# A fused retention and ELU layer: the last 2048 tokens in two blocks of 1024 instead of four of 512, with the first weight's pieces streamed from DRAM

## The chip, the cores and the metric

The kernel runs on one core of a Trainium2 chip. The metric is device time in microseconds (us) of one execution; lower is better. All engines work through queues of instructions in order: TensorE (PE, with its weight loads PEld), VectorE (DVE), ScalarE (ACT), GpSimd (POOL) and SyncE (SP), which here issues all the DMAs.

## The reference

Retention over 4 batches, 8 heads, 768 positions and 64 dimensions, then a layer of two products with an ELU between them, all in fp32:

```python
gamma = 1.0 - 2.0 ** (-5.0 - np.arange(H))
for t in range(S):
    state = gamma * state + einsum('bhd,bhe->bhde', k[:, :, t], v[:, :, t])
    y[:, :, t] = scale * einsum('bhd,bhde->bhe', q[:, :, t], state)
x = y.transpose(0, 2, 1, 3).reshape(3072, 512)
h = x @ w_in                                # 512 x 2048
g = where(h > 0, h, exp(min(h, 0)) - 1)
out = g @ w_out                             # 2048 x 512
```

## The kernel before

**Blocks.** The 3072 tokens are worked off in six blocks of 512 (`tb` 0 to 5). For each, the retention gives x (in chunks of 128 tokens: `scores`, `states`, `outputs_step`, gathered in `retention_step`, with small 64x64 matmuls), then come the "first" (x @ w_in and ELU) and the "second" (g @ w_out). The two products are done after Strassen and Winograd: seven products of half-size blocks instead of eight, with sums of blocks before (on DVE) and after (on ACT, which copies a product out of PSUM, and DVE, which adds the next to it). Block 0 is done plainly at first, block 1 has a one-level first (`first`, products L758). For blocks 2 to 5 (loop L1363) the first is one-level in five of its seven products (`first_rest`, L923, 256 columns) and two-level in two of them, j = 2 and 3 (`first_twice`, L870, 128 columns). The second of blocks 1 to 5 is two-level throughout (`second_twice`, L953): seven outer products in the order 1, 2, 6, 7, 5, 3, 4 (`ORDER2`), each with seven inner ones of four matmuls 128 columns wide (L973).

**Weights.** Blocks and sums of w_in lie in SBUF to the end (`w_a`, `w_b`, `w_s`); `first_rest` reads them there. The 49 pieces of w_out and the four sums for each of j = 2, 3 of w_in are computed once, stored to DRAM scratch, and fetched again for each block as pieces of 128x512 (256 KB) into a ring of 11 tiles named `wq` (`fetch_small`, L809): whenever a product has used its piece, the next fetch is issued on SP. The ring is opened after the staging tiles `stage` (named `wi` where sums are staged) are closed, in the same SBUF space. The sums of w_in are made by `combine_small` (L833) during block 1's first, and each j is stored by one DMA of 1 MB (L657, `send_small`).

**Order.** The order of the instructions is written by hand. Work of the next block (chunk loads `bring`, the scaling of v L286, the retention steps, x combinations L468) is put between the products of the current one; the second's last products are left as a `tail` to the next block's first. ELU (`elu`, L491 to L495) is Relu and Exp on ACT and one operation on DVE, which `later` defers. A DMA on SP waits for the one eight DMAs earlier.

**Steps touched.** `lift` and `plus` (L895, L899) take the two-level products out of PSUM, `first_end` (L939) adds and starts the ELU, `next_input` (L782 ff.) builds the second's inputs in place, `input_parts` makes the four differences of each outer product (L847), and `sum_up` adds outer products and stores the output.

Of the kernel before, what the change touches and what calls it, by code (L numbers as in the profile page):

```python
# [18 lines left out]
def kernel(  # L19
# [6 lines left out]
    scratch3: bass.AP,  # L26
    out: bass.AP,
# [47 lines left out]
    mpool = ctx.enter_context(tc.tile_pool(name="mpool", bufs=4))  # L75
    hpool = ctx.enter_context(tc.tile_pool(name="hpool", bufs=4))
    epool = ctx.enter_context(tc.tile_pool(name="epool", bufs=2))
    small = ctx.enter_context(tc.tile_pool(name="small", bufs=6))
# [5 lines left out]
    stage = early.enter_context(tc.tile_pool(name="stage", bufs=3))  # L84
    t4 = early.enter_context(tc.tile_pool(name="t4", bufs=1))
# [188 lines left out]
    x_of = lambda tb: xt_.rearrange("p j a t -> p j (a t)") if tb == 1 else xb  # L274
# [516 lines left out]
    RING = 11  # L791
    TWICE = [2, 3]
    SMALL = {5: 0, 6: 1, 7: 2, 3: 3}
    small_w, to_fetch, before = [], [], []
    for tb in range(1, NTB):
        for j in TWICE if tb > 1 else []:
            m1, m2, *mine = [(tb, 0, j, k) for k in (1, 2, 6, 7, 5, 4, 3)]
            to_fetch += [m1] + before[:1] + [m2] + mine[:2] + before[1:] + mine[2:3]
            before = mine[3:]
        to_fetch, before = to_fetch + before, []  # L800
        for j in ORDER2:
            last = (4, 3) if j == 4 and tb == NTB - 1 else (3, 4)
            mine = [(tb, 1, j, k) for k in (1, 2, 6, 7, 5) + last]
            to_fetch += mine[:2] + before + mine[2:5]
            before = mine[5:]
        to_fetch, before = to_fetch + before, []
    to_fetch = [x for x in to_fetch if x[1] == 1 or x[3] in SMALL]

    def fetch_small():  # L809
        if not to_fetch:  # L810
            return
        name = to_fetch.pop(0)
        _, which, j, k = name
        t = ring.tile([P, 4, P], FP32, name="wq", tag="wq")
        if k in SMALL:
            n = SMALL[k]
            nc.sync.dma_start(
                t.rearrange("p f d -> p (f d)"), (scratch2[SEVEN[j]] if which else scratch3[j - 1])[:, 512 * n : 512 * n + 512]
            )
        else:  # L820
            q = 4 * SLOT[j] + {1: 0, 2: 1, 4: 3}[k]
            nc.sync.dma_start(t.rearrange("p f d -> p (f d)"), scratch[q])
        small_w.append((name, t))


    W_IN = {2: w_a_[:, :, :, 1], 3: w_s_[:, :, 2]}

    def combine_small(j):

        t = stage.tile([P, 4, 4, P], FP32, name="wi", tag="stage")  # L830
        a11, a12, a21, a22 = (W_IN[j][:, 2 * r : 2 * r + 2, :, c, :] for r in range(2) for c in range(2))
        s1, s2, s3, s4 = (t[:, k].rearrange("p (n f) c -> p n f c", f=2) for k in range(4))
        tt = lambda o, x, y, op: nc.vector.tensor_tensor(out=o, in0=x, in1=y, op=op)  # L833
        tt(s1, a21, a22, ALU.add)
        yield
        tt(s2, s1, a11, ALU.subtract)
        yield
        tt(s3, a11, a21, ALU.subtract)
        yield
        tt(s4, a12, s2, ALU.subtract)  # L840
        to_send.append((scratch3[j - 1], t.rearrange("p k f d -> p (k f d)")))
# [3 lines left out]
    def quarters_of_input(t, b11, b12, b21, b22):  # L845

        sub = lambda o, x, y: nc.vector.tensor_tensor(out=o, in0=x, in1=y, op=ALU.subtract)  # L847
        sub(t[:, 0], b12, b11)
        yield
        sub(t[:, 1], b22, t[:, 0])  # L850
        yield
        sub(t[:, 2], b22, b12)
        yield
        sub(t[:, 3], b21, t[:, 1])

    def combine_x_twice():

        t = tpool.tile([P, 4, 2, 2, P], FP32, name="ts", tag="ts")
        b = [xb[:, 2 + k].rearrange("p (h t c) -> p t h c", h=2, t=2)[:, u] for k in range(2) for u in range(2)]
        for _ in quarters_of_input(t[:, :, 0], *b):  # L860
            pass
        for n, j in enumerate(TWICE):
            b11, b12, b21, b22 = (x[:, n] for x in b)
            s1, s2, s3, s4 = (t[:, k, 0, n] for k in range(4))
            xs[j] = {1: b11, 2: b21, 3: b22, 4: s4, 5: s1, 6: s2, 7: s3}


    PLACE = {2: "C11", 3: "C12"}

    def first_twice(tb, j):  # L870

        dst = PLACE[j]
        place = lambda name, r, t: gq[name][:, 4 * r : 4 * r + 4, P * t : P * t + P]
        full = lambda t: t.rearrange("p a (b c) -> p (a b) c", c=P)

        def product(k, ps, begin):
            if k in SMALL:
                name, w = small_w.pop(0)
                assert name == (tb, 0, j, k)
                lhs = [w[:, f, :] for f in range(4)]  # L880
            else:
                r, c = {1: (0, 0), 2: (0, 1), 4: (1, 1)}[k]
                lhs = [W_IN[j][:, 2 * r + f // 2, f % 2, c, :] for f in range(4)]
            for f in range(4):
                nc.tensor.matmul(  # L885
                    ps[:, f, :], lhsT=lhs[f], rhs=xs[j][k], start=(begin and f == 0), stop=True,
                    skip_group_check=True,
                )
            if k in SMALL:
                fetch_small()  # L890

        def lift(ps, o=None):
            if o is None:
                o = full(mpool.tile([P, 2, TH], FP32, name="m", tag="m"))
            nc.scalar.copy(o, ps)  # L895
            return o

        def plus(r, t, ps, m):
            nc.vector.tensor_tensor(out=place(dst, r, t), in0=ps, in1=m, op=ALU.add)  # L899

        pa = full(bank("a"))
        product(1, pa, True)
        m1 = lift(pa)
        yield
        pb = full(bank("b"))
        product(2, pb, True)
        plus(0, 0, pb, m1)
        product(6, pa, False)
        u2 = lift(pa)
        pd = full(bank("d"))  # L910
        product(7, pd, True)
        m7 = lift(pd)
        yield
        product(5, pa, False)
        plus(1, 1, pa, m7)
        yield
        product(4, pd, False)
        plus(1, 0, pd, u2)
        yield
        product(3, pa, False)  # L920
        lift(pa, place(dst, 0, 1))

    def first_rest(n, j, ps):  # L923

        w, x = {
            1: (w_a[n][:, :, 0], xb[:, 0:2, half[0]]), 6: (w_s[n][:, 0], xt[1]), 5: (w_b[n][:, :, 0], xt[0]),
            4: (w_b[n][:, :, 1], xt[3]), 7: (w_s[n][:, 1], xt[2]),
        }[j]
        for fi in range(2):
            for j2 in range(2):  # L930
                nc.tensor.matmul(  # L931
                    ps[:, fi, :], lhsT=w[:, fi, j2, :], rhs=x[:, j2, :],
                    start=(j in (1, 7) and fi == 0 and j2 == 0), stop=(j2 == 1), skip_group_check=True,
                )

    def first_end(n, name, ps, x=None):

        g = gq[name][:, 2 * n : 2 * n + 2, :]
        nc.vector.tensor_tensor(out=g, in0=ps, in1=g if x is None else x, op=ALU.add)  # L939
        g = g.rearrange("p a b -> p (a b)")  # L940

        def combine():
            mine = lambda x: gq[x][:, 2 * n : 2 * n + 2, :].rearrange("p a b -> p (a b)")
            sub = lambda o, x, y: nc.vector.tensor_tensor(out=o, in0=x, in1=y, op=ALU.subtract)
            sub(mine("T3"), mine("C22"), mine("C12"))
            if n < NQ - 1:
                sub(mine("T1"), mine("C12"), mine("C11"))
            else:
                later.append(lambda: sub(mine("T1"), mine("C12"), mine("C11")))

        return lambda: elu(g, g, 3, combine if name == "C22" else None)

    def second_twice(tb, behind_last):  # L953
# [7 lines left out]
        def input_parts(j):  # L961
            x, t = gq[INPUT2[j]], tpool.tile([P, 4, 4, P], FP32, name="ts", tag="ts")
# [6 lines left out]
        def product(j, k, ps, begin):  # L969
            name, w = small_w.pop(0)  # L970
            assert name == (tb, 1, j, k)
# [5 lines left out]
            fetch_small()  # L977
# [34 lines left out]
        def inner_end(j):  # L1012

            res = hpool.tile([P, 2, 2, P], FP32, name="res", tag="h")
            to = out[tb, 1, 0].rearrange("p d (t c) -> p d t c", t=2)
            k = kept2[7].rearrange("p (d t c) -> p d t c", d=2, t=2)
            pa = bank("a")[:, 0, 0:P]
            product(j, 1, pa, True)
            m1 = copy(pa)
            pb = bank("b")[:, 0, 0:P]  # L1020
            product(j, 2, pb, True)
            add(res[:, 0, 0], pb, m1)
            yield
            product(j, 6, pa, False)
            u2 = copy(pa)
            pd = bank("d")[:, 0, 0:P]
            product(j, 7, pd, True)
            m7 = copy(pd)
            yield
            add(u2, u2, k[:, 1, 0])  # L1030
            add(u2, pd, u2)
# [479 lines left out]
```

## Time and profile before

| | |
|---|---|
| three runs | 632.44 to 634.4 us, median 634.11 us |
| profiled execution, span | 631.6 us |
| DVE, ACT, POOL busy | 76%, 40%, 4% of the span |
| moved by DMA | 136.32 MB, 216 GB/s in the mean |
| pieces `wq` fetched | 277 of 256 KB, landing 4.4 us after issue |
| chunks fetched | 22 of 1 MB, landing 8.7 us after issue |

A line of the timeline has the start, the time to the end of the last instruction, engine, line, operation, output <- input, tile shapes and number of instructions. An fp32 matmul leaves two records. "gC" and "ts" are the input blocks of the second and their sums, pa to pd are PSUM banks; `gT` is the tile of T3.

### The profile page before, as it was taken

To read this page: it belongs to the slowest core of one execution; us is meant where nothing else is said; L and a number is where in the kernel's file an instruction comes from. 1 tells how busy PE (TensorE), PEld (TensorE's weight loads), DVE (VectorE), ACT (ScalarE), POOL (GpSimd) and SP (SyncE) were. 2 spreads that over 40 slices of the span, in tenths; PEclk is the share of its full clock that TensorE was granted. 3 is DMA by queue.
4 is the path that set the end of the run, shared out by engine and by line. 5 is a ranking of instruction groups with operands and counts; after the bars stand their busy time and mean duration, and the time that the engine had idled before them with its cause. 6 is when DMAs were issued, how large, how long until landed. Compare 5 with 4: busy or idle time off the path is not lost.

```text
span 631.6 us, 16140 instructions
## 1 busy us (share of the span) xinstructions
PE 623.8 (99%) x6678; PEld 560.5 (89%) x6678; DVE 482.1 (76%) x882; ACT 255.3 (40%) x476; POOL 22.1 (4%) x30
## 2 busy tenths in 40 slices
PE   8999999999999999999999999999999999999997
PEld 6864578888899999888999989999989999988997
DVE  6688789989799665799585589777489877558975
ACT  6798646025541114553112646112465211366311
POOL 1021000000000000200000100000110000000000
PEclk9999999999999999999999999999999999999999
DMA  8698669699288788306888702889810698700794
GB/s 329 260 416 295 186 202 268 196 272 319 113 266 257 234 258 315 141 2 199 257 258 296 278 2 71 268 280 289 317 64 16 220 310 252 207 17 4 239 309 151
DMA packets 75897, 136.32 MB, mean 216 GB/s; under 512 B 6320, under 2 KB 31792, under 8 KB 70832
## 3 DMA queue, kind: packets, MB, share of 16 engines
q1 hardware_dynamic: 75824, 135.29, 64.9%
q8 instruction: 53, 0.87, 0.5%
q14 instruction: 20, 0.16, 0.1%
HBM read 114.03 MB, written 21.23 MB: 214 GB/s over the span
## 4 chain that ended last, share of the span: by engine, by line
PE 98%; DVE 0%; issue 0%; ACT 0%
PE pa L973 20%; PE pa L931 10%; PE pd L973 10%; PE pb L973 5%; PE pa L885 5%; PE pb L931 4%; PE pa L758 4%; PE pa L535 3%; PE qa L931 3%; PE x L625 3%; PE pd L885 2%; PE qd L931 2%; PE pd L931 2%; PE pd L758 2%; PE pa L625 2%; PE kv L352 2%
## 5 line engine op out<-in xcount | busy, mean ns | idle before, releaser
L981 ACT COPY ms<-pa 128x128 f32<-128x128 f32 x104 | 27.6, 265 | 148.2 <-PE pa L973 148.2
L973 PE MATMUL pa<-ts,wq 128*128 128x128 f32 x560 | 74.2, 275 | 0.0
L973 PE MATMUL pd<-ts,wq 128*128 128x128 f32 x552 | 73.5, 276 | 0.0
L973 PEld LDWEIGHTS pa<-ts,wq 128*128 128x128 f32 x560 | 68.5, 192 | 0.4
L973 PEld LDWEIGHTS pd<-ts,wq 128*128 128x128 f32 x552 | 67.1, 192 | 0.6 <-DVE res L985 0.2
L973 PE MATMUL pa<-gC,wq 128*128 128x128 f32 x480 | 64.6, 278 | 0.0
L492 ACT ACTIVATE r<-r 128x512 f32<-128x512 f32 x96 | 60.5, 631 | 3.1
L973 PEld LDWEIGHTS pa<-gC,wq 128*128 128x128 f32 x480 | 59.0, 192 | 1.3
L491 ACT ACTIVATE r<-gC 128x512 f32<-128x512 f32 x64 | 39.9, 624 | 31.9 <-DVE gC L939 31.9
L985 DVE TENSOR_TENSOR res<-pd,ms 128x128 f32<-128x128 f32 x68 | 19.5, 287 | 39.6 <-PE pd L973 38.4
L495 DVE SCALAR_TENSOR_TENSOR gC<-r,gC 128x512 f32<-128x512 f32 x64 | 42.6, 697 | 0.7 <-ACT r L492 0.7
L847 DVE TENSOR_TENSOR ts<-gC,ts 128x512 f32<-128x512 f32 x60 | 41.3, 688 | 1.0
L847 DVE TENSOR_TENSOR ts<-gC 128x512 f32<-128x512 f32 x60 | 41.0, 683 | 0.0
L286 POOL TENSOR_TENSOR chunk<-chunk,vf 128x512 f32<-128x512 f32 x16 | 19.4, 1212 | 429.6 <-DMA chunk<-in_qkv_dram 429.6
L973 PE MATMUL pb<-gC,wq 128*128 128x128 f32 x240 | 31.7, 275 | 0.0
L1006 ACT COPY res<-pa 128x128 f32<-128x128 f32 x34 | 9.0, 265 | 55.1 <-PE pa L973 55.1
L973 PEld LDWEIGHTS pb<-gC,wq 128*128 128x128 f32 x240 | 29.2, 192 | 0.0
L704 ACT COPY m<-pa 128x512 f32<-128x512 f32 x24 | 14.0, 582 | 33.0 <-PE pa L758 18.7
L939 DVE TENSOR_TENSOR gC<-qa,gC 128x512 f32<-128x512 f32 x8 | 5.5, 692 | 25.0 <-PE qa L931 18.3
L931 PE MATMUL pa<-xt,w_s 128*128 128x256 f32 x96 | 23.0, 382 | 0.0
L931 PE MATMUL pa<-xt,w_b 128*128 128x256 f32 x96 | 23.0, 382 | 0.0
L931 PE MATMUL pa<-xb,w_a 128*128 128x256 f32 x96 | 22.7, 379 | 0.0
(262 smaller groups left out, 1247.4 us busy)
## 6 DMA issues: line engine op xcount, KB each, us to landing
wq<-scratch_dram SPq DMA_DIRECT2D x277, 256.0 KB, 4.4
chunk<-in_qkv_dram SPq DMA_DIRECT2D x22, 1024.0 KB, 8.7
wraw<-in_w_dram SPq DMA_DIRECT2D x15, 1024.0 KB, 6.0
out_dram<-res SPq DMA_DIRECT2D x14, 256.0 KB, 4.1
scratch_dram<-gT SPq DMA_DIRECT2D x12, 256.0 KB, 4.3
scratch_dram<-m SPq DMA_DIRECT2D x12, 192.0 KB, 6.1
scratch_dram<-so SPq DMA_DIRECT2D x4, 512.0 KB, 4.7
scratch_dram<-wi SPq DMA_DIRECT2D x2, 1024.0 KB, 6.5
```

Of the source, the lines that this page charges most:

```text
L286: eng.tensor_tensor(out=v, in0=v, in1=vf[:, i].unsqueeze(2).to_broadcast([C, H, D]), op=ALU.mult)
L491: nc.scalar.activation(e, h, AF.Relu, scale=-1.0)
L492: nc.scalar.activation(e, e, AF.Exp, scale=-1.0)
L495: nc.vector.scalar_tensor_tensor(g, e, -1.0, h, ALU.add, ALU.max)
L625: nc.tensor.matmul(X[j][:, d, :], lhsT=w[j][:, d * P : d * P + P], rhs=x[j], start=(n == 0 and d == 0), stop=at_end, skip_group_check=True,)
L758: nc.tensor.matmul(ps[:, fi, :], lhsT=w[:, fi, j2, :], rhs=x[:, j2, :], start=(begin and fi == 0 and j2 == 0), stop=(j2 == 1), skip_group_ ...
L847: sub = lambda o, x, y: nc.vector.tensor_tensor(out=o, in0=x, in1=y, op=ALU.subtract)
L885: nc.tensor.matmul(ps[:, f, :], lhsT=lhs[f], rhs=xs[j][k], start=(begin and f == 0), stop=True, skip_group_check=True,)
L931: nc.tensor.matmul(ps[:, fi, :], lhsT=w[:, fi, j2, :], rhs=x[:, j2, :], start=(j in (1, 7) and fi == 0 and j2 == 0), stop=(j2 == 1), skip_ ...
L973: nc.tensor.matmul(ps, lhsT=w[:, f, :], rhs=ts[j][k][:, f, :], start=(begin and f == 0), stop=(f == 3), skip_group_check=True,)
L981: nc.scalar.copy(m, ps)
L985: nc.vector.tensor_tensor(out=o, in0=x, in1=y, op=ALU.add)
```

## The change

Blocks 2, 3 and blocks 4, 5 are merged to two blocks of 1024 tokens (`NB` = 2). In them the second's matmuls are 256 columns wide (`second_big`), the two-level products of the first also (`big_twice`, four passes in the order of `ORDER1`), and its other five products 512 (`big_rest`).

The larger tiles need room. So w_in no longer stays in SBUF: during block 1's first, all pieces of it are stored to DRAM (`send_quarters`: twelve DMAs of 128 KB; `send_layer`: twenty of 256 KB; `combine_small` sends six DMAs for each j instead of one), and `w_a`, `w_b`, `w_s` become tiles for g (`G`). All weights of the large blocks are then fetched as pieces from `scratch3`, `scratch4` and the scratches of w_out, into a ring of 8 slots (for block 1's second 14). The pools `mpool`, `hpool`, `small` are closed after block 1 and two larger ones opened.

Block 1's second runs to its end before the first large block begins. The retention steps lie at other places (`VISITS`): block 3's are inside two passes of `big_twice`, blocks 4 and 5 inside the first `second_big`; chunks of blocks 3 and 5 are loaded four at once. The output's layout changes, and the host puts it in order.

```diff
-    RING = 11
-    TWICE = [2, 3]
...
+    def fetch():
+        while wanted and slots:
+            name, source = wanted.popleft()
+            slot = slots.popleft()
+            nc.sync.dma_start(slot[:, 0 : source.shape[1]], source)
+            where[name] = slot
+
+    def done(name):
+        slot = where.pop(name)
+        if slot in kept_slots or wanted and wanted[0][0][0] == 1:
+            slots.append(slot)
+        fetch()
...
-        to_send.append((scratch3[j - 1], t.rearrange("p k f d -> p (k f d)")))
+        for at in range(2):
+            to = scratch3[j - 2, at]
+            mine = t[:, :, 2 * at : 2 * at + 2].rearrange("p k f d -> p k (f d)")
+            to_send.append((to[1].rearrange("p (k c) -> p k c", k=2), mine[:, 1:3]))
+            to_send.append((to[2][:, 0:256], mine[:, 0]))
+            to_send.append((to[3][:, 0:256], mine[:, 3]))
+
+    def send_quarters(j):
+
+        for at in range(2):
+            for k, n, half in ((1, 0, 0), (2, 0, 1), (4, 2, 1)):
+                r, c = {1: (0, 0), 2: (0, 1), 4: (1, 1)}[k]
+                to_send.append((
+                    scratch3[j - 2, at, n][:, 256 * half : 256 * half + 256].rearrange("p (f d) -> p f d", f=2),
+                    W_IN[j][:, 2 * r + at, :, c, :],
+                ))
...
+    def send_layer(j, ns):
+
+        for n in ns:
+            to_send.append((
+                scratch4[PLANE[j], n].rearrange("p (f c) -> p f c", f=2), LAYER[j][:, n].rearrange("p f k c -> p f (k c)")
+            ))
...
+    def big_layer_x():
+
+        sub = lambda o, x, y: nc.vector.tensor_tensor(out=o, in0=x, in1=y, op=ALU.subtract)
+        b11, b12, b21, b22 = (x[:, 2 * r : 2 * r + 2] for r in range(2) for x in (xa, xb2))
+        t1, t2, t3, t4_ = (next_ts().rearrange("p (k t) -> p k t", k=2) for _ in range(4))
+        layer_x.update({1: b11, 5: t1, 6: t2, 7: t3, 4: t4_})
+        sub(t1, b12, b11)
+        yield
+        sub(t2, b22, t1)
+        yield
+        sub(t3, b22, b12)
+        yield
+        sub(t4_, b21, t2)
...
+    def big_twice(n, j, at):
...
+            for f in range(2):
+                nc.tensor.matmul(
+                    ps[:, f, :], lhsT=w[:, f * P : f * P + P], rhs=big_xs[j][k], start=(begin and f == 0), stop=True,
+                    skip_group_check=True,
+                )
+            if half or k == 3:
+                done(name)
...
+        pa = bank("a")
+        product(1, pa, True)
+        m1 = lift(pa)
+        yield
+        pb = bank("b")
+        product(2, pb, True)
+        plus(0, 0, pb, m1)
+        product(6, pa, False)
+        u2 = lift(pa)
+        pd = bank("d")
+        product(7, pd, True)
+        m7 = lift(pd)
+        yield
+        product(5, pa, False)
+        plus(1, 1, pa, m7)
...
+    def big_end(m, name, ps, x=None):
+
+        g = G[name][m // 4][:, m % 4, :]
+        nc.vector.tensor_tensor(out=g, in0=flat(ps), in1=g if x is None else flat(x), op=ALU.add)
...
+    def next_big_input(j):
+
+        x, op = {2: ("T3", ALU.add), 6: ("C21", ALU.subtract)}[j]
+        for r in range(2):
+            for q in (slice(0, 2), slice(2, 4)):
+                nc.vector.tensor_tensor(out=G["C11"][r][:, q], in0=G[x][r][:, q], in1=G["C11"][r][:, q], op=op)
...
@@ -1331,15 +1553,34 @@
+        if n == 0:
+            send_quarters(2)
+            send_layer(1, range(NQ))
+            send_layer(4, range(NQ))
+        elif n == 1:
+            for j in (6, 7, 5):
+                send_layer(j, range(NQ))
+            send_quarters(3)
         send_small()
...
-    for _ in range(RING):
-        fetch_small()
-
-    sec = second_twice(1, combine_x_twice)
+    ring_ = ctx.enter_context(tc.tile_pool(name="ring", bufs=1, side="right")).tile([P, 8, 512], FP32, name="wq")
...
+    fetch()
+
+    sec = second_twice(1, lambda: run(big_x(2)))
...
+    for nb in range(NB):
...
+        for at, (j, sub) in enumerate(ORDER1):
+            if at == 2:
+                rest(0, 1)
+            cur = big_twice(nb, j, sub)
             next(cur)
-            next(tail, None)
-            next(parts, None)
+            if at:
+                next(tail, None)
+            else:
+                run(tail)
             next(cur)
...
+            if at == 0 and nb == 0:
+                retention_step(3, 0)
+            elif at == 1:
+                if nb == 0:
+                    retention_step(3, 2)
+                    next(tail)
+                    retention_step(3, 3)
+                    for _ in tail:
+                        pass
+                    retention_step(3, 4)
+                some(xparts, 4)
+            elif at == 2:
+                some(xparts, 2)
+                if more:
+                    bring(groups[0], 0)
+            elif at == 3:
+                run(xparts)
+                if more:
+                    bring(groups[0], 1)
+            if at == 2:
+                big_end(0, "C11", qa[0])()
...
+        VISITS = [(0, "end"), (1, "middle"), (1, "end"), (3, "end"), (4, "middle"), (4, "end"), (5, "middle"), (5, "end")]
         for s in sec:
...
+            if more and at in VISITS:
+                n = VISITS.index(at)
+                if n < 3:
+                    retention_step(groups[0], n + 2)
+                    if n == 1:
+                        for m in range(CPB):
+                            bring(groups[1], m)
+                else:
+                    retention_step(groups[1], n - 3)
```

## The prediction

> **What bounds the kernel now.** I read the page from the top: busy shares, slices, chain, groups; then stretches of the trace where the change works. First the shares and the chain of waits that ended last.
>
> ```profile
> PE 623.8 (99%) x6678; PEld 560.5 (89%) x6678; DVE 482.1 (76%) x882; ACT 255.3 (40%) x476; POOL 22.1 (4%) x30
> PEclk9999999999999999999999999999999999999999
> PE 98%; DVE 0%; issue 0%; ACT 0%
> ```
>
> TensorE is busy for 623.8 of 631.6 us at full clock, and the chain is TensorE all the way. So a gain must be time of PE itself, and any wait put into PE's queue is paid in full. Next, PE's pitch. The means of one in the groups (275 ns at 128 columns, 382 ns at 256) overlap their neighbours and can't be divided; the timeline gives starts of whole products.
>
> ```profile
> 190.51 1.06 PE L973 MATMUL pd<-ts,wq 128*128 128x128 f32 x8
> 191.40 1.06 PE L973 MATMUL pa<-ts,wq 128*128 128x128 f32 x8
> ...
> 132.64 1.89 PE L758 MATMUL pa<-xt,w_a 128*128 128x256 f32 x8
> 134.37 1.89 PE L758 MATMUL pb<-xt,w_a 128*128 128x256 f32 x8
> ...
> 37.31 3.60 PE L535 MATMUL pa<-xb,w_a 128*128 128x512 f32 x8
> 40.74 3.60 PE L535 MATMUL pa<-xb,w_b 128*128 128x512 f32 x8
> ```
>
> Eight records are four matmuls. Start to start: 0.893 us, so 223.3 ns each at 128 columns; 1.727 us, 431.6 ns at 256; 3.43 us, 858 ns at 512. Twice the width costs 1.93 and 1.99 times as much: wide matmuls save only the small rest.
>
> **What the change removes.** Per pair of blocks the two-level second goes from 2x196 matmuls of 128 columns to 196 of 256; for four blocks 784 become 392, each saving 2x223.3-431.6 = 15.0 ns: 5.9 us. The two-level products of the first (224 become 112) save 1.7 us, its other five products (320x431.6 become 160x858) 0.8 us. Together 8.4 us. The largest idle of PE before, 1.25 us at 298 us in L423 (an output product of the retention), is at a place that is rearranged: taken as gone. A gain of 9.7 us; bounds 8.4 and 9.7. DVE and ACT work half as many, twice as wide operations; that would be a gain only if they bounded.
>
> The Trainium skill, page "TensorE: Matmul & The Clock Gate", section Back-to-back issue gap, gives for sustained streams about 81 ns a matmul at 128 columns and 131 at 512. By that (98 at 256, an estimate) the 175 us of 784 narrow products would shrink by some 69 us; the 223.3 and 431.6 ns above contradict the ratio, and the measurement decides.
>
> **What it adds: a later first fetch (step A).** Pieces for the stages after it can be fetched only when the ring's tiles, which overlie the staging tiles, are free, so when the last store from `wi` has landed. The queue before:
>
> ```profile
> 146.50 0.47 SPq L110 DMA_DIRECT2D chunk<-in_qkv_dram  x1
> 147.66 0.33 SPq L657 DMA_DIRECT2D scratch_dram<-wi  x1
> 148.10 1.09 SPq L110 DMA_DIRECT2D chunk<-in_qkv_dram  x2
> 168.19 0.33 SPq L657 DMA_DIRECT2D scratch_dram<-wi  x1
> 173.33 0.80 SPq L822 DMA_DIRECT2D wq<-scratch_dram  x2
> ...
> 177.53 1.05 PE L973 MATMUL pa<-gC,wq 128*128 128x128 f32 x8
> ```
>
> And what the DMA engines moved, in slices of 1.425 us from 125 us:
>
> ```profile
> GB/s 290 285 285 284 287 335 116 210 318 230 351 289 349 179 236 284 228 276 247 443 425 414 431 414 109 0 0 0 0 0 98 379 264 12 65 338 286 236 346 404
> ```
>
> The bytes run out at about 159.3 us; the last `wi` leaves at 168.19 (its inputs on DVE, L833, end then) and takes until about 173.1; the first fetch, issued at 173.33, can have landed at about 175.5, and PE wants it at 177.53. The changed queue has, ahead of that fetch, 12 quarter stores of 128 KB and 20 layer stores of 256 KB more: 1.57+5.24 = 6.8 MB, while the two 1 MB `wi` stores become six each. At 350 GB/s these take 19.4 us. Cover: 8.9 us idle (159.3 to 168.2), 1.8 us because the last `wi` overlaps others instead of running alone, 2.0 us of slack on PE. So PE stalls 19.4-12.7 = 6.7, say 7 us. The rate is not shown for this mix: 425 GB/s (the chunk loads at 152 to 158) would give 3.3 us; 258 GB/s (eight DMAs in flight of 192 KB landing in 6.1 us, the row scratch<-m) 13.7. Most bytes are 256 KB stores, landing in 4.3 us (gT), nearer the first: 350. Behind the late SP queue also stand two chunk loads, whose scaling (L286) waits on DVE; that lies under the same PE stall.
>
> The page "DMA: Bandwidth & Descriptors", sections Bandwidth and Rules for kernel authors, asks for 1 MiB a DMA and measures 138 GB/s at 64 KB against 341 at 1 MB, so it speaks against cutting the stores. At 200 GB/s, an estimate between, the 6.8 MB would be 34 us and the stall 21.
>
> **Small ones.** Chunk loads come four at once (4.2 MB, 9.9 us at 425 GB/s) where they came singly. With 13 pieces ahead of block 3's at 0.893 us each, 11.6 us, less 2 us of landing: 0.6 us short; for block 5's seven pieces of 1.73 us, 12.1 us, are enough. 0.6 (0 to 4). The handover where pools are closed: 0.25 (0 to 0.5). The retention of block 3, four steps within one pass instead of over a block: the next products wait for DVE's scaling of y (L398): 0.8 (0 to 1.5). The last sum and store, 128x512 for 128x128: 0.5.
>
> **Step E: the fourth pass of `big_twice`.** Before, the ELU of the first C11 follows all lifts on ACT, and only x combinations of 512 columns stand beside it:
>
> ```profile
> 244.33 0.68 DVE L468 TENSOR_TENSOR xt<-xb,xt 128x512 f32<-128x512 f32 x1
> 246.60 0.69 DVE L939 TENSOR_TENSOR gC<-qa,gC 128x512 f32<-128x512 f32 x1 [1.59 <-ACT gC L895]
> ...
> 245.98 0.58 ACT L895 COPY gC<-pa 128x512 f32<-128x512 f32 x1 [0.31 <-PE pa L885]
> 247.32 0.63 ACT L491 ACTIVATE r<-gC 128x512 f32<-128x512 f32 x1 [0.76 <-DVE gC L939]
> 247.99 0.63 ACT L492 ACTIVATE r<-r 128x512 f32<-128x512 f32 x1
> ```
>
> Now DVE has, in this order: plus(1,1) of the third pass; two subtractions of `big_layer_x` (128x1024); C11's add (`big_end`). ACT has behind that add its Relu and Exp, and only then the lift of m1 of the fourth pass, which PE's product 6 needs to reuse the bank. With t=0 where product 5 of the third pass ends: DVE 0.7 + 2x1.13 + 0.7 = 3.7 us (from 128x128 0.287, 128x256 0.42, 128x512 0.685 a column step of 1.04 ns is read, 1.13 spaced for 1024), ACT 2x0.63+0.58 and handovers to 5.7. PE has three products for that time (1, 4, 2), 6x431.6 ns = 2.6 us. Stall 3.1, in both blocks: 6.2 us (5 to 7). Nothing stands behind it that PE could do; DVE catches up in it.
>
> **Step F: `second_big` of the first block with retention inside.** At product 2 the `seen` copy stands behind four `next_big_input` sums (4x1.13 against 3.5 us of PE work): 0.4. At product 5 the state sums go at the middle, behind four sums and half the input parts: 2.0. At product 3 the `across` matmuls wait behind three dependent 128x1024 sums (1.25 each) and four subtractions: 2.0. Together 4.4 (2 to 6). Before, the same sums were 0.7 us and retention stood at other places.
>
> **Sum.** 631.6-9.7+7.0+0.6+0.25+0.8+6.2+4.4+0.5 = 641.7 as a span. The profiled execution is 2.5 us under the median 634.1, so as a run **644 us**.
>
> **Rivals.**
> (1) Faster: the stores drain at 425 GB/s and the DVE and ACT waits of E and F hide. For it: the DMA engines were idle 9 us here and DVE is busy 76% only. Against: E's chain is in order on two queues, so half of it at the least must go by a wrong duration. With A 3.3 and half of E, F and of the small ones: 634.1-9.7+3.3+5.3+1.1 = 634.1; with A nil, E and F at a fifth and the small ones at half: 627.6. It ends faster only if A+E+F come to less than 6 us.
> (2) DMA decides: small stores at 258 GB/s (A 13.7), chunk bursts 4 us late: 644+6.7+3.4 = 654. For it: 192 KB stores landing in 6.1 us. Against: 256 KB in 4.3.
> (3) No change: gain and waits cancel, A 3.3 with E and F at half, 634 as above.
> (4) The wide matmuls don't gain what is said, because a 256-column product is held up by its piece, 256 KB in 1.73 us (152 GB/s); then 644+8.4 = 652. Before, 261 GB/s ran beside the 128-column products from 180 to 200 us with PE busy for 20.00 of 20.00 us, so hardly.
>
> **How the numbers follow.** This kernel's three runs span 0.3%, so the bound for a change that can be told is 0.3%, 1.9 us: 632.2 to 636.0. Forecast and its neighbourhood (636 to 650): 0.62; rival 2 and 4: 0.10; rival 3: 0.10; rival 1: 0.18. Slower 0.72, same 0.10, faster 0.18. Range 631 to 652: it lets out most of rival 1 and the worst of rival 2.
>
> **What would show it.** A: the first 128-column product of the two-level second in block 1 waits for a DMA, PE idle 3 to 14 us near 178. E: PE idle about 3 us at product 6 of the fourth pass, twice, ACT's lift of m1 behind Relu and Exp. F: idle of 2 us before y products in the first large second. Products of 256 columns at 1.73 us each. I am wrong if the first fetch lands before 178, or if DVE at 128x1024 is shorter than 1.1 us.

## The result, and the profile after

| | before | after |
|---|---|---|
| median of four runs each, same chip | 633.52 us (632.44 to 634.40) | 657.99 us (655.32 to 659.90) |
| ratio, 95% interval | | 1.0392 (1.0359 to 1.0425): slower |
| span of the profiled execution | 631.6 us | 654.8 us |
| PE busy | 623.8 us | 623.8 us |
| moved by DMA | 136.32 MB | 126.67 MB |

The direction was forecast, the size was not: 24.5 us slower, where the forecast of 644 was 10 above the median known then, and the time lies outside the range of 631 to 652. The page of the changed kernel, first the shares, the clock in 40 slices and the chain of waits:

```profile
PE 623.8 (95%) x5350; PEld 469.5 (72%) x5350; DVE 470.8 (72%) x730; ACT 245.9 (38%) x420; POOL 24.4 (4%) x30
PEclk9999999999969989989999999999999999999999
PE 85%; DVE 6%; DMA 6%; issue 1%; SPq 1%; ACT 1%; DVEq 0%; ACTq 0%
```

The chain is no longer PE alone: DVE and DMA have 6% each. PE is idle for 31.0 us (654.8-623.8), before 7.8. And the clock, full throughout before, has three slices below 9. The timeline of PE shows where (the number in brackets is the idle time before the line and what ended it):

```profile
176.43 1.89 PE L761 MATMUL pa<-xb,w_b 128*128 128x256 f32 x8
188.17 2.05 PE L911 MATMUL pa<-gC,wq 128*128 128x128 f32 x8 [9.85 <-DMA wq<-scratch_dram]
190.01 1.92 PE L911 MATMUL pb<-gC,wq 128*128 128x128 f32 x8
...
235.74 1.33 PE L911 MATMUL pa<-w_a,wq 128*128 128x128 f32 x8 [2.85 <-DMA wq<-scratch_dram]
236.86 1.92 PE L911 MATMUL pa<-gC,wq 128*128 128x128 f32 x8
...
288.13 2.08 PE L1111 MATMUL pa<-ts,wq 128*128 128x256 f32 x4 [2.97 <-ACT m L1121]
405.09 1.99 PE L1202 MATMUL pa<-gC,wq 128*128 128x256 f32 x8 [0.80 <-DMA wq<-scratch_dram]
435.44 1.55 PE L411 MATMUL y<-chunk 64*64 64x64 f32 x62 [1.48 <-DVE chunk L367]
453.80 0.69 PE L426 MATMUL y<-chunk 64*64 64x64 f32 x32 [1.62 <-DVE seen L395]
494.01 1.13 PE L1111 MATMUL pa<-ts,wq 128*128 128x256 f32 x4 [2.91 <-ACT m L1121]
```

These seven waits add up to 22.5 us, and the steps A (188), chunk loads (235, 405), E (288, 494) and F (435, 454) are all there. Not foreseen is what follows some of them: from 188.17 to 190.01 four matmuls of 128 columns take 1.84 us, twice the 0.893 of before. The view by stretches gives PE's busy time (second number), and after the engines the clock, the DMA share and GB/s:

```profile
186.00:188.00 2.00, 0.00 (x0) 0.00 (x0) 1.03 (x2) 0.00 (x0) 0.00 (x0) 0.50 0.71 259
188.00:190.00 2.00, 1.83 (x8) 1.86 (x9) 0.00 (x0) 0.00 (x0) 0.00 (x0) 0.50 0.73 181
190.00:192.00 2.00, 2.00 (x11) 2.00 (x10) 0.00 (x0) 0.27 (x1) 0.00 (x0) 0.50 0.96 239
192.00:194.00 2.00, 2.00 (x10) 1.70 (x10) 0.89 (x2) 0.14 (x1) 0.00 (x0) 0.96 1.00 373
```

After the wait PE works at half clock for nearly 4 us; the clock had fallen near 182 us, during the wait. Summed over stretches of 2 us, PE's busy time times the missing share of clock comes to 5.2 us: 2.0 after 188 us, 1.7 after 235, 1.5 after 288. After 494 the clock stayed at 1.00.

### The profile page after: what moved, and what is told of

Same layout as the page of the kernel before. It is cut to its first block, busy times and chain, and to the rows that moved or that the text cites. A ratio compares the mean times of both kernels' runs of the same rounds, so it can differ in the third digit from the quotient of the medians.

```text
span 654.8 us, 13105 instructions
## 1 busy us (share of the span) xinstructions
PE 623.8 (95%) x5350; PEld 469.5 (72%) x5350; DVE 470.8 (72%) x730; ACT 245.9 (38%) x420; POOL 24.4 (4%) x30
## 2 busy tenths in 40 slices
DMA packets 76010, 126.67 MB, mean 193 GB/s; under 512 B 5936, under 2 KB 40496, under 8 KB 71216
## 4 chain that ended last, share of the span: by engine, by line
PE 85%; DVE 6%; DMA 6%; issue 1%; SPq 1%; ACT 1%; DVEq 0%; ACTq 0%
PE pa L1202 13%; PE pa L1154 11%; PE pd L1202 6%; DMA wq<-scratch_dram 5%; PE pa L1111 4%; PE pb L1154 4%; PE pa L761 4%; PE pb L1202 4%; PE pa L538 3%; PE x L628 3%; PE pd L1154 3%; PE pa L911 3%; PE pa L628 2%; PE pd L1111 2%; PE y L411 2%; PE pd L761 2%
## 5 line engine op out<-in xcount | busy, mean ns | idle before, releaser
L1202 PE MATMUL pd<-ts,wq 128*128 128x256 f32 x120 | 28.3, 379 | 0.0
L1202 PE MATMUL pa<-gC,wq 128*128 128x256 f32 x112 | 26.8, 382 | 0.8 <-DMA wq<-scratch_dram 0.8
L1202 PE MATMUL pa<-ts,wq 128*128 128x256 f32 x112 | 26.7, 381 | 0.0
L1154 PE MATMUL pa<-ts,wq 128*128 128x512 f32 x56 | 26.5, 596 | 0.0
L1154 PE MATMUL pa<-xt,wq 128*128 128x512 f32 x56 | 26.3, 592 | 0.0
L1154 PE MATMUL pa<-w_s,wq 128*128 128x512 f32 x56 | 26.3, 592 | 0.0
L707 ACT COPY m<-pa 128x512 f32<-128x512 f32 x26 | 15.1, 582 | 29.4 <-PE pa L761 18.8
L1202 PEld LDWEIGHTS pd<-ts,wq 128*128 128x128 f32 x120 | 22.8, 190 | 3.1
L1202 PEld LDWEIGHTS pa<-gC,wq 128*128 128x128 f32 x112 | 21.0, 190 | 4.5 <-DMA wq<-scratch_dram 1.2
L1111 PE MATMUL pa<-ts,wq 128*128 128x256 f32 x64 | 18.1, 407 | 5.9 <-ACT m L1121 5.9
L1202 PEld LDWEIGHTS pa<-ts,wq 128*128 128x128 f32 x112 | 21.1, 190 | 3.4 <-issue 0.5
L911 PE MATMUL pa<-gC,wq 128*128 128x128 f32 x72 | 11.6, 312 | 10.2 <-DMA wq<-scratch_dram 9.8
```

The source lines that it names most:

```text
L707: nc.scalar.copy(m, ps)
L911: nc.tensor.matmul(ps, lhsT=w[:, f, :], rhs=ts[j][k][:, f, :], start=(begin and f == 0), stop=(f == 3), skip_group_check=True,)
L1111: nc.tensor.matmul(ps[:, f, :], lhsT=w[:, f * P : f * P + P], rhs=big_xs[j][k], start=(begin and f == 0), stop=True, skip_group_check=True,)
L1154: nc.tensor.matmul(flat(ps), lhsT=w[:, k, :], rhs=layer_x[j][:, k, :], start=(j in (1, 7) and k == 0), stop=(k == 1), skip_group_check=True,)
L1202: nc.tensor.matmul(ps, lhsT=w[:, f, :], rhs=ts[j][k][:, f, :], start=(begin and f == 0), stop=(f == 3), skip_group_check=True,)
```

## The experiments

Three things had to be told apart: whether the waits come from where the prediction put them, whether the half clock comes from the waits and costs what it seems to, and whether the wide matmuls gain anything once the waits are gone. The ratio behind each is against the kernel before on the same chip.

**1. The stores alone, in the kernel before.** The extra 32 stores are added at the changed kernel's places; `fetch_small`, the ring and the narrow matmuls stay.

```diff
+        if n == 0:
+            send_quarters(2)
+            send_layer(1, range(NQ))
+            send_layer(4, range(NQ))
+        elif n == 1:
+            for j in (6, 7, 5):
+                send_layer(j, range(NQ))
+            send_quarters(3)
         send_small()
```

> The kernel before, with the change's 32 extra stores of w_in (6.8 MB) put at the same places of the queue, and nothing else; what they store is never read. Theory (the stores hold back the first fetch): in the changed kernel PE idled 9.85 us there and then ran some 4 us at a clock of 0.50, so about 2 us more; here 633.5+12 = 645 us, PE idle 8 to 11 us near 178 us, and a fetch as what ends it. Rival (the new ring and its tiles, or the changed places of retention, hold back the first product; stores pass in the idle time of the DMA engines): 633 to 635 us, no idle there.

Measured: 644.73 us, ratio 1.0181 (1.0161 to 1.0200). Its PE timeline, and SP's at the same place:

```profile
176.40 1.89 PE L760 MATMUL pa<-xb,w_b 128*128 128x256 f32 x8
188.71 2.05 PE L995 MATMUL pa<-gC,wq 128*128 128x128 f32 x8 [10.41 <-DMA wq<-scratch_dram]
...
174.97 0.38 SPq L659 DMA_DIRECT2D scratch_dram<-wi  x1
185.47 0.80 SPq L824 DMA_DIRECT2D wq<-scratch_dram  x2
```

The stores alone make the wait, 10.41 us, and 11.9 us of time (632.87 us was the median of before beside it), as expected; neither the changed ring and pools nor the moved retention is needed for it. The first fetch leaves at 185.47 us, before at 173.33.

**2. The first C11's ELU behind the lifts.**

```diff
             elif at == 2:
-                some(xparts, 2)
+                elu_later = big_end(0, "C11", qa[0])
+                some(xparts, 1)
...
             elif at == 3:
+                elu_later()
                 run(xparts)
...
-            if at == 2:
-                big_end(0, "C11", qa[0])()
```

(The second wide difference moves into the fourth pass.)

> The changed kernel with the first C11's add and ELU moved behind the lifts of the fourth pass of the two-level first, and the two 1024-wide x differences there set apart. Theory (that ELU stands ahead of the lift of m1 in ACT's queue): the two waits of 2.97 and 2.91 us near 287 and 493 us go, and the half clock after the first (1.5 us) with them: 7 us less than the changed kernel's 658, 651 us. Rival (the bank is late because of DVE's wide differences, whatever ACT does): the waits stay within 1 us of what they were, 656 to 658.

Measured: 650.74 us, ratio 1.0276 (1.0248 to 1.0303). In ACT's timeline of the changed kernel the lift stands behind Relu and Exp, which stand behind DVE's add:

```profile
286.31 0.63 ACT L494 ACTIVATE r<-w_a 128x512 f32<-128x512 f32 x1 [4.01 <-DVE w_a L1164]
286.97 0.63 ACT L495 ACTIVATE r<-r 128x512 f32<-128x512 f32 x1
287.51 0.57 ACT L1121 COPY m<-pa 128x512 f32<-128x512 f32 x1
```

With the ELU moved, the same lift comes first, and product 6 follows product 2 at PE's own pitch:

```profile
287.23 0.58 ACT L1121 COPY m<-pa 128x512 f32<-128x512 f32 x1 [1.22 <-PE pa L1111]
...
287.83 1.03 PE L1111 MATMUL pb<-xb,wq 128*128 128x256 f32 x4
288.70 1.03 PE L1111 MATMUL pa<-ts,wq 128*128 128x256 f32 x4
```

Both waits are gone; 7.25 us between the medians. The edit moved one wide difference as well, so the time alone does not separate the ELU from the rival of DVE's wide differences. The rows do: the lift itself waits only for PE's product (PE pa above), and in the changed kernel it came last because Relu and Exp stood ahead of it on ACT, held by DVE's add. DVE's wide differences act through that add, not by themselves.

**3. Chunk loads one at a time.**

```diff
-                        for m in range(CPB):
-                            bring(groups[1], m)
...
+            singly = [(1, "middle"), (2, "first"), (2, "middle"), (3, "first")]
+            if more and at in singly:
+                bring(groups[1], singly.index(at))
```

(And block 3's loads likewise, one at the middle of each of the third to sixth outer products.)

> The changed kernel with the chunk loads of blocks 3 and 5 issued one at a time, over four places each, instead of four at once. Theory (4.2 MB at once hold back the pieces behind them): the wait of 2.85 us near 234 us and that of 0.80 us near 404 us go, and about 1.7 us of half clock after the first: 5 us less, 653 us. Rival (the ring of 14 slots is too short for a piece in 0.893 us whatever stands between): the wait near 234 us moves but stays over 2 us, 656 to 658.

Measured: 656.79 us, ratio 1.0367 (1.0331 to 1.0403), which does not separate it from the changed kernel. The waits for pieces near 235 and 405 us are gone, as the theory says, so the ring was not too short. But a new one of 1.97 us came near 417 us: block 5's scores, for its last chunk (L315). That, a first wait of 10.27 us in this execution instead of 9.85, and 0.7 us more of half clock behind it gave some 3 of the 5 us back.

**4. PE kept busy through the first wait.**

```diff
+    def keep_busy(count):
+        for n in range(count):
+            nc.tensor.matmul(fill, lhsT=line[:, 0:P], rhs=line[:, P : P + 512], start=True, stop=True, skip_group_check=True)
...
+    keep_busy(11)
```

> The changed kernel with 11 matmuls of 512 columns (11x0.858 = 9.4 us) on constants, read by nobody, put on PE just ahead of the first product that waits for a piece near 178 us. Theory (after an idle time PE runs at half clock for a while): the wait is then filled, the granted clock near 188 to 192 us is 1.00, and the time falls by some 2 us, to 656. Rival (the clock falls at that place for another reason, the load on DMA or memory): clock 0.50 at 188 to 192 us again, and no gain: 658.

Measured: 658.98 us, ratio 1.0410 (1.0382 to 1.0438), no gain.

```profile
178.70 9.61 PE L1588 MATMUL fill<-etab 128*128 128x512 f32 x22
189.40 1.13 PE L911 MATMUL pa<-gC,wq 128*128 128x128 f32 x8 [1.10 <-DMA wq<-scratch_dram]
190.37 1.06 PE L911 MATMUL pb<-gC,wq 128*128 128x128 f32 x8
```

The clock was 1.00 from 184 to 194 us and the products had their pitch of 0.89 us or little more, so it is PE's idling that lowers the clock; the rival is out. From the end of the product ahead of the wait to the third product of L911 16.0 us pass (178.70 to 194.72), in the changed kernel 17.2 (178.16 to 195.39), though the first piece came 0.7 us later here: locally the two microseconds are there. The time of the whole does not show them. This trace has breaks of 0.32, 0.34 and 1.38 us inside products at 202.7, 207.8 and 214.4 us, for which the profile names no releaser, and they come to as much; whether they follow from the filler or from chance stays open. The long one began at 213.01 us, 0.89 us after a 16 KB transfer of the DMA queue for instructions had started, and the break of 1.25 us in the kernel before 0.98 us after one. That points to PE running out of instructions, but it is not shown: most such transfers are followed by no break.

**5. PE kept busy at the lift** (the same three-line helper, `keep_busy(3)` ahead of product 6 of the fourth pass).

> The changed kernel with three matmuls of 512 columns on constants (2.6 us) ahead of product 6 of the fourth two-level pass of each large block, where PE waits 2.9 us for ACT's lift. In the changed kernel 9.89 us pass in the first large block from the start of product 2 of that pass (284.13 us) to the next 512-column product (294.02 us), with the clock at 0.50 to 0.72 from 288 to 292. Theory (the clock falls because PE idles; where pieces are at hand, the slow matmuls are paid in full): clock 1.00 there and 8.4 us between the same two products. Rival (the slow clock costs nothing because something else sets the pace): 9.9 us again.

Measured (one run, 654.34 us): 283.61 to 292.04 us, 8.43 us, as the theory says, with the clock at 1.00 throughout: the slow clock was paid in full there, 1.5 us. The trace of experiment 4 has the same case without a filler: by chance the clock stayed at 1.00 there after the same wait of 2.97 us, and the stretch took 8.42 us (285.49 to 293.91).

**6. Most layer stores later.** 14 of 20 layer stores go out with the products of the first `big_twice` passes; the ring of block 1's second loses four slots, since `w_b` is needed longer.

```diff
-            send_layer(4, range(NQ))
+            send_layer(4, range(1))
         elif n == 1:
-            for j in (6, 7, 5):
-                send_layer(j, range(NQ))
+            send_layer(5, range(1))
             send_quarters(3)
...
+            send_some(2)
```

> The changed kernel with 14 layer stores and 4 quarters' worth less ahead of the first fetch: of the 20 layer stores only six (layer 1, and the first of layers 4 and 5) stay there, the other 14 (3.7 MB) go out during the two-level passes of the first large block, two with each product; the ring of block 1's second has 10 slots for 14. Theory (every byte of store ahead of the first fetch delays it): 3.7 MB at some 350 GB/s are 10.5 us, so the wait of 9.85 us near 178 us all but goes, and the 2 us of half clock with it; the chunk burst near 234 us costs up to 4 us more with 4 slots less. 658-12+2 = 648, range 645 to 652. Rival (stores only move the wait: what is sent later delays the pieces of the large block as much): 655 or more, with PE waiting for DMA between 255 and 300 us.

Measured: 653.14 us, ratio 1.0319 (1.0304 to 1.0334); between theory and rival.

```profile
176.97 1.89 PE L761 MATMUL pa<-xb,w_b 128*128 128x256 f32 x8
178.86 1.13 PE L911 MATMUL pa<-gC,wq 128*128 128x128 f32 x8
...
217.04 1.06 PE L911 MATMUL pb<-gC,wq 128*128 128x128 f32 x8
225.61 2.05 PE L911 MATMUL pa<-gT,w_b 128*128 128x128 f32 x8 [7.52 <-DMA w_b<-scratch_dram]
```

The wait near 178 us is gone. But the burst of four chunk loads, with ten slots ahead of it for fourteen, now costs 7.52 us instead of 2.85, and half clock after it. Not the later stores took over, as the rival had it (PE waits for no piece between 255 and 300 us), but the next stall in line, which was to cost up to 4 us more and cost 4.7.

**7. Block 5's retention at other places.**

```diff
-        VISITS = [(0, "end"), (1, "middle"), (1, "end"), (3, "end"), (4, "middle"), (4, "end"), (5, "middle"), (5, "end")]
+        VISITS = [(0, "end"), (1, "middle"), (1, "end"), (3, "end"), (4, "first"), (4, "end"), (5, "middle"), (6, "middle")]
```

> The changed kernel with block 5's retention at other places in the first large second: the state sums ahead of the second input's wide sums, and the last step one place later. Theory (products of y wait behind DVE's 128x1024 sums): the waits of 1.48 us near 435 and 1.62 us near 453 us fall under 0.5 us each: 2.5 us less, 655.5. Rival (y waits for PE's own kv and score products or for PSUM banks): waits as before, 658.

Measured: 654.77 us, the median of three runs (649.49 to 656.84; a fourth took 660.29), ratio 1.0332 (1.0293 to 1.0371). The waits of 1.48 and 1.62 us are not in its trace any more, so the theory holds for these two places; its runs scatter too much for the time to say it.

**8. All repairs together** (2, 3, 6 and 7, with block 5's chunk loads one or two places earlier than in 3).

> All repairs together: stores later (ring of 10 slots), chunk loads singly, the first C11's ELU behind the lifts, and the retention of block 5 at places that are not behind the wide sums (states ahead of them, the last step one place later). Theory (the wide matmuls gain 8.4 us and the rest was waits that the order of the queues made): the waits of 9.85, 2.85, 2.97, 2.91, 1.48 and 1.62 us go and with them 5 us of half clock: 658-27 = 631, between 626 and 635, PE clock 1.00 throughout and PE idle under 12 us. Rival (one wait takes the place of another: with fewer slots and bytes moved, PE waits for pieces elsewhere): 638 or more.

Measured: 633.68 us over twelve runs, ratio 1.0010 (0.9994 to 1.0025).

```profile
span 629.8 us, 13111 instructions
PE 616.8 (98%) x5350; PEld 464.1 (74%) x5350; DVE 469.4 (75%) x730; ACT 245.8 (39%) x420; POOL 23.0 (4%) x30
PEclk9999999999999999999999999999999999999999
```

The clock is full again, and PE's busy time is 7.0 us under before: that is the gain of the wide matmuls, at last visible. Of it 5.2 us are given back in idle time (13.0 us for 7.8), in waits of at most 0.74 us after the start. The profiled execution is the fastest of the twelve; by the medians nothing is won.

**9. The same with 12 slots.**

> All repairs together as before, with two of the four layer pairs of w_b stored early in place of one, so that block 1's second has 12 slots for 10. Theory (what is left of waits in the kernel with all repairs, some 1.7 us for pieces between 224 and 240 us, comes from the short ring): these go, no wait comes back near 178 us, and the time falls by 1 to 2 us to 632, just under the kernel before. Rival (0.5 MB more of stores bring the wait near 178 us back): 1.5 us idle there, 633.5 to 635.

Measured: 632.44 us, ratio 0.9994 (0.9982 to 1.0005). The waits for pieces between 224 and 240 us are gone, but a wait of 2.11 us stands ahead of the first product of L911 again (180.36 us). The profile puts its end down to DVE's ELU (L498), which ended at 180.20 us; the first piece had landed only 0.14 us before. In experiment 8 the same product began ahead of that ELU, so the piece is the likelier cause. A version that beats the kernel before was not found; this one equals it.

**10. v scaled by DVE in place of POOL.**

```diff
-        eng = nc.vector if by_vector or m < 2 else nc.gpsimd
+        eng = nc.vector if by_vector or m < 2 or m >= 4 * CPB else nc.gpsimd
```

> The changed kernel with v of blocks 4 and 5 scaled by DVE in place of POOL. In the changed kernel three of DVE's 128x1024 operations between 399 and 407 us took 1.95 to 2.06 us where 1.22 is the rule, and POOL was at a scaling of v during each of them. Theory (POOL's and DVE's operations hinder each other): none of them takes more than 1.3 us here. Rival (the 9.9 us of chunk transfers into SBUF slow DVE): still about 2 us.

Measured (one run): 681.98 us. None of DVE's 128x1024 sums and differences took more than 1.23 us, but DVE's queue now stood behind the chunk transfers (the scaling waited 6.43 us for the first), and PE behind DVE: waits of 5.13, 3.67 and 8.81 us at 294, 331 and 418 us. So it does not separate theory and rival by itself: the sums no longer ran while chunks came in. The last section has a row that does.

## Why the prediction was wrong

The forecast sum was a span of 641.7 us, 13.1 us under the 654.8 measured. Three parts make it: idle time of PE rose by 23.2 us where 19.75 added and 1.25 removed were forecast (4.7 us); the clock cost 5.2 us, for which the sum had no term; and PE's busy time at full clock fell by 5.2 us (623.8 to 623.8-5.2) where 8.4 were forecast (3.2 us). From the span to the median run 2.5 us were added, and it is 3.2 (657.99-654.8).

- **Gain.** The pitches were right: 1.727 us for four matmuls of 256 columns, 1.717 for two of 512. In the kernel with all repairs 7.0 us of 8.4 are seen. Of the 3.2 us missing in the changed kernel 1.8 are in the retention: from start to start, without the idle times shown, the y products (L411 and L426) of blocks 2 to 5 took 18.8 us, 17.0 before. The rest is not placed. The 1.25 us break at L423, taken as gone, did go, but breaks of that kind came elsewhere in experiments 4 (1.38 us) and 6 (1.47 us), so this part of the gain may be luck.
- **A, 7 us: 9.85, within its bounds.** The place, the cause and what the wait ends with were right, and experiment 1 shows them alone. The rate was too high: the first fetch was forecast for 173.33+19.4-8.9-1.8 = 182.0 us and left at 185.47, so the 6.8 MB behaved as at 298 GB/s (6.8/22.8), nearer the lower bound than the 350 taken.
- **Chunk loads, 0.6 us: 3.65 (2.85+0.80).** This is the step that failed in its reasoning. (Its own terms, 11.6-2 against 9.9 us, give 0.3 and not 0.6.) It let the four chunks have the DMA engines to themselves for 9.9 us. SP's issues, and the stretch from the first chunk's issue to the end of PE's wait (last number: GB/s):

```profile
220.67 2.71 SPq L113 DMA_DIRECT2D chunk<-in_qkv_dram  x4
...
220.67:235.74 15.07, 12.22 (x133) 11.99 (x125) 12.04 (x20) 1.86 (x7) 4.94 (x4) 1.00 0.96 352
```

At 352 GB/s the engines moved 5.3 MB in these 15.07 us: the chunks' 4.2 and pieces beside them. Experiments 3 and 6 confirm it from both sides: none with single loads, 7.52 with four slots less.
- **E, 6.2 us: 5.88.** 5.8 us from the end of product 5 (282.32) to product 6 (288.13), where 5.7 were worked out from in-order queues and durations. 128x1024 took 1.22 us at a spacing of 1.13, as extrapolated.
- **F, 4.4 us: 3.1.** The waits at outer products 5 and 3 came as 1.48 and 1.62 us for 2.0 each; at product 2 none for the `seen` copy (0.4 in the sum, though its terms, 4x1.13 against 3.5 us, give 1.0).
- **Handover, block 3's retention, last store, 1.55 us: about 2.0.** This is what is left: 8.5 us of idle time outside the seven waits, less 6.5 before without its 1.25. No run separates the three.
- **Clock: 0 in the sum, 5.2 us.** This is the other step that failed, and the largest single error: the sum priced PE's stalls as if PE ran at full clock after them. The trace of before could not show it: its longest idle time amid the work was 1.25 us, with the clock at 1.00. The Trainium skill, "TensorE: Matmul & The Clock Gate", section "HAM oscillation — how this bites in real kernels", does warn of idle times over some 3.4 us and of half clock after them; by it at least A, priced at 7 us, should have carried that. Runs here agree in the half clock, and show it after shorter waits too, of 2.32 us in experiment 2.

Of the rivals the second, where DMA decides, came nearest with 654 us. Its mechanisms were the right ones and its 4.0 us for the chunk bursts was close, but its 13.7 us for A (9.85 measured) stood in for the clock's 5.2, so that it came near is in part luck. The range held one bound at a time, and stopped at 652 though the errors of all steps that wait for DMA go the same way.

## What to carry to other kernels

Where PE is the bound and every queue is in order, a gain of 1 or 2% in matmul shape is easily lost to the order of stores, chunk loads and lifts: the same wide kernel took 658 us in one order and 632 in another. A wait of PE of over 2 us can bring the slow clock behind it, and from 3.6 us on it always did here: price it. After a stall is removed, recompute the next one: with the four slots less in the ring that the first one's repair cost, the second was 4.7 us longer.

## What the hardware showed that was not expected

**The clock after a wait.** Over the traces of this study, PE's waits of up to 2.11 us amid the work (after 100 us) never lowered the clock, and all of 3.6 us and more did. Between 2.3 and 3.0 us, 8 of 15 did: the wait of 2.91 us near 491 us lowered it in some executions and not in others, and one of 2.32 us did. It then stood at 0.50 for 3 to 6 us of work, sometimes from about a microsecond after the restart.

What decides is where the wait lies. Within each trace the granted clock changes only on a grid of 3.41 us (the half-clock stretches amid the work are 3.41, 6.83, 10.24 or 13.65 us long), and the grid lies differently against the program from one execution to the next. Steps of the grid around the waits for the lift, two pairs from the changed kernel, then one each from experiments 4 and 3 (the second number is PE's busy time, the clock is the third from the end):

```profile
284.31:287.72 3.41, 0.84 (x4) 0.39 (x3) 2.50 (x4) 1.38 (x3) 1.04 (x1) 1.00 0.79 281
287.72:291.13 3.41, 3.00 (x7) 2.46 (x8) 0.69 (x1) 0.94 (x2) 0.00 (x0) 0.50 0.01 3
489.11:492.52 3.41, 1.99 (x10) 1.41 (x8) 3.41 (x5) 0.33 (x1) 0.00 (x0) 1.00 0.31 106
492.52:495.94 3.42, 1.93 (x9) 1.72 (x10) 0.87 (x2) 1.99 (x4) 0.00 (x0) 1.00 0.18 61
...
285.11:288.52 3.41, 1.40 (x7) 0.90 (x5) 3.06 (x4) 0.82 (x2) 0.00 (x0) 1.00 0.96 339
288.52:291.94 3.42, 2.45 (x11) 2.20 (x12) 0.69 (x1) 1.92 (x4) 1.04 (x1) 1.00 0.09 33
...
284.99:288.40 3.41, 1.39 (x6) 1.25 (x7) 1.41 (x3) 1.95 (x4) 1.04 (x1) 1.00 0.39 122
288.40:291.82 3.42, 3.42 (x9) 2.70 (x8) 0.00 (x0) 1.54 (x3) 0.00 (x0) 0.50 0.26 77
```

The wait of 2.97 us near 285 lay almost whole within one step and the next step ran at half clock; the wait of 2.91 us near 491 was shared by two steps and cost nothing. Over all twelve traces, after 100 us, each of the 29 full-clock steps with 2.02 us or more of idle time of PE (21 amid the work, the others at the end) was followed by half clock, and none of the 1848 with 2.01 us or less. Near 10 us, in the first retention, 1.4 to 1.8 us were enough in three executions, so idle time is not the whole measure. The page named above, section "What's actually happening", explains it by an activity window that runs free of the program, which fits this grid.

**POOL and DVE.** In the changed kernel some DVE operations took longer by about the length of a POOL operation. DVE and POOL there, from their timelines:

```profile
401.59 1.21 DVE L881 TENSOR_TENSOR ts<-gC 128x1024 f32<-128x1024 f32 x1
402.83 1.95 DVE L881 TENSOR_TENSOR ts<-gT,ts 128x1024 f32<-128x1024 f32 x1
404.70 2.06 DVE L881 TENSOR_TENSOR w_s<-gT,gC 128x1024 f32<-128x1024 f32 x1
406.69 1.21 DVE L881 TENSOR_TENSOR w_s<-gT,ts 128x1024 f32<-128x1024 f32 x1
...
402.05 1.65 POOL L289 TENSOR_TENSOR chunk<-chunk,vf 128x512 f32<-128x512 f32 x1 [1.47 <-DMA chunk<-in_qkv_dram]
404.54 1.15 POOL L289 TENSOR_TENSOR chunk<-chunk,vf 128x512 f32<-128x512 f32 x1 [0.83 <-DMA chunk<-in_qkv_dram]
```

The POOL line reads, like DVE's, two operands from SBUF. That DMA is not the cause shows at 227.94 and 228.54 us: two DVE operations of 128x512 took 0.68 us each, their usual time, the first wholly between two POOL scalings, the second begun there, and with DMA at 418 GB/s, while the one at 226.60, begun in the middle of a scaling, took 1.42 (another, begun together with that scaling at 225.89, took 0.68; there the scaling was the longer one, 1.59 us where 1.04 is the least). The skill's page "SBUF — State Buffer", section "Who interferes with whom", has it that a DVE instruction with two SBUF inputs contends with a GpSimd instruction that reads SBUF; these rows agree.
